# Linear attention and a SoLU feed-forward layer in one kernel: the first tile's hidden layer in float32, the maxima of k spread through DRAM, and a new order list

## The chip, the cores and the metric

The kernel runs on one core of one Trainium2 chip. The metric is the device time of one execution in microseconds, as the median over runs. Five engines work side by side and each executes its own instructions strictly in the order in which the kernel recorded them: PE (TensorE, matmuls), DVE (VectorE), ACT (ScalarE), POOL (GpSimd) and SP, which in this kernel only starts transfers. Engines wait for one another by semaphores. An instruction that waits holds up everything behind it on its own engine.

## The reference

```python
# attention; b, h, s, d = 8, 8, 576, 64
q_s = softmax(q, axis=-1)            # over d, with + 1e-9 in the denominator
k_s = softmax(k, axis=2)             # over the sequence: needs the maximum of k over s
kv  = einsum('bhsd,bhse->bhde', k_s, v)
out = einsum('bhsd,bhde->bhse', q_s, kv)

# feed-forward on x = out as [4608, 512]; d_ff = 1024
h    = x @ w_in
e    = exp(h - max(h)); sm = e / (sum(e) + 1e-9)
solu = h * sm
ln   = (solu - mean(solu)) / sqrt(var(solu) + 1e-6) * g_ln
y    = ln @ w_out
```

## The kernel before

The 4608 rows are 36 row tiles of 128: four from the first 512 rows of each batch, `(b, 0)` to `(b, 3)`, and one, `(b, 4)`, for every odd b, from the 64 remaining rows of two batches. All work is written as generators that yield between small steps.

For a batch b, `keys(b)` (key `K`) takes the maximum of k over the sequence: pairwise maxima on DVE (`khalf`, `ktop`), four float32 transposes on PE (`turned`), a reduction on DVE (`col`, a column of 128 x 4 numbers: the maximum for each of the 512 head and feature pairs). `col` must then reach all 128 partitions. Four more transposes of a broadcast `col` on PE (`wide`) and a copy on ACT (`kb`) do that. Then `km - kb` in two halves of heads and `kr - kb` for the last 64 rows (POOL, or DVE where the order list says so), exp on ACT, the float32 products k^T v on PE (`kv`, L386 and L391), a normalisation, and a split into a high and a low float16 part (`bd`). `queries(b, ...)` (`Qba`, `Qbc`) makes the softmax of q, its high and low part `qhl`, and a transposed copy `qT` by a DMA transpose from SP.

For a row tile, `attend` (`x`) multiplies `bd` and `qT` on PE and splits the result into float16 parts `xT` (high on ACT, low on DVE). `hidden` (`h`) multiplies with the high and low parts of `w_in` (`wi`): three float16 products for each of four blocks of 128 and each of two halves, 24 matmuls of 128x512. The maximum `top` (DVE, L550), exp `e` (ACT), `h*e` (DVE), mean, the high and low parts `u` and their transpose `uT` (a DMA transpose from SP), and the variance follow. `project` (`o`) multiplies `uT` with `wo`, 24 more matmuls, and stores.

The weights arrive as float64 words. `weight_in` (`w`) turns them into float32 `iw`; `weights_in_scaled` (`W`) takes the maximum of the column sums through PE (`wide_in`), makes a power of two, `s_in`, and writes the four blocks of `wi` (high on ACT, low on DVE, L280). `weight_out` (`y`) and `weights_out_scaled` (`Z`) do the same for `wo` (L321). `P` is a warm-up: four matmuls on idle data.

What sets the order is `ORDER`, a list of keys written out in one string. Each key advances its generator by one step; `.v` gives that step to DVE instead of its usual engine, and `*n` repeats it. So the list fixes the order on all engines, SP included, and the engine of the steps that have a choice. PSUM holds two `h` tiles, three of the tag "att" (`turned`, `wide`, `kv`, `x`) and one `o`. Number suffixes in the names below are buffers: `xT0_2` belongs to tile (0, 2), `kb2` to batch 2.

Of the kernel before, what the change touches and what calls it, by code (L numbers as in the profile page):

```python
# [8 lines left out]
F32 = mybir.dt.float32  # L9
# [8 lines left out]
P = 128  # L18

BUFS = 12, 4, 2  # L20
ORDER = (
# [77 lines left out]
def linear_attention_solu_ffn(ctx: ExitStack, tc: tile.TileContext, q, k, v, w_in, w_out, g_ln, out):  # L99
# [13 lines left out]
    C = 4  # L113
# [42 lines left out]
    def cast(eng, out, x):  # L156
        if eng is nc.scalar:
            eng.copy(out, x)  # L158
        else:
            eng.tensor_copy(out, x)  # L160

    def largest(x, wide, name):

        nc.tensor.transpose(wide, x.broadcast_to([P, P]), ident)
# [572 lines left out]
```

## Time and profile before

| | us |
|---|---|
| median of 3 runs (lowest to highest) | 475.32 (474.86 to 476.75) |
| the profiled execution, its own time | 477.42 |
| its span from first to last instruction | 475.6 |
| around the span | 1.8 |
| PE, DVE, ACT, POOL busy | 445.4, 342.7, 283.5, 208.8 |

A duration of a matmul in the profile includes its way through the array, and matmuls overlap. What one costs the engine is the distance from its start to the next start. In the tables of stages, the granted clock of PE is 1.00 at full speed and 0.50 at half.

### The profile page before, as it was taken

Reading aid. Unit: us, or ns where it says so; the run is one execution under the profiler, and the core shown is the slowest. Engines: PE = TensorE matmul, PEld = TensorE weight load, DVE = VectorE, ACT = ScalarE, POOL = GpSimd, SP = SyncE. Lnnn points to the kernel's source line nnn. Section 1 sums busy time; section 2 is a strip of 40 time slices with the busy share of each in tenths; the row PEclk is TensorE's granted clock in tenths of the full one; section 3 lists DMA queues with packets and bytes.
Section 4 is the critical chain, followed back from the end, with each engine's and each line's share of the span. In section 5 each row is a group of like instructions: output and inputs, shape, how many; then the busy total and the mean of one; then the engine's idle time right before and its main releaser. Section 6 shows DMA issues by size and latency. Waiting matters only on the chain.

```text
span 475.6 us, 8323 instructions
## 1 busy us (share of the span) xinstructions
PE 445.4 (94%) x3150; PEld 224.3 (47%) x3150; DVE 342.7 (72%) x596; ACT 283.5 (60%) x472; POOL 208.8 (44%) x308
## 2 busy tenths in 40 slices
PE   4367989999999999999899999999999999999997
PEld 1243444455445445544454454645454444444454
DVE  3989999979988898768888877656787655531610
ACT  1687899777657676845564657575575365441420
POOL 3222595395849526742742346541664411121210
PEclk9555999999999999999999999999999999999999
DMA  8899979198898878498729952959434462351062
GB/s 260 263 269 289 237 194 233 36 245 154 216 191 170 198 205 158 75 239 184 180 65 251 221 126 52 212 140 219 111 74 91 81 134 68 73 104 45 12 145 88
DMA packets 159240, 74.99 MB, mean 158 GB/s; under 512 B 127840, under 2 KB 152672, under 8 KB 159200
## 3 DMA queue, kind: packets, MB, share of 16 engines
q1 hardware_dynamic: 159200, 74.47, 67.1%
q8 instruction: 24, 0.39, 0.3%
q14 instruction: 16, 0.13, 0.1%
HBM read 36.70 MB, written 9.44 MB: 97 GB/s over the span
## 4 chain that ended last, share of the span: by engine, by line
PE 77%; DVE 7%; DMA 7%; ACT 4%; issue 2%; SPq 2%; POOL 1%; DVEq 0%; ACTq 0%
PE o L617 35%; PE h L543 33%; PE x L519 3%; PE kv L386 3%; DMA qT<-qhl 3%; DMA w_in<-in_moe_w_in_dram 2%; DMA km<-in_k_dram 2%; DVE top L550 1%; DVE gw L253 1%; PE wide L339 1%; DVE u L579 1%; PE kv L391 1%; DMA v<-in_v_dram 1%; PE turned L332 1%; ACT e L586 1%
## 5 line engine op out<-in xcount | busy, mean ns | idle before, releaser
L543 PE MATMUL h<-wi,xT 128*128 128x512 f16 x864 | 200.7, 381 | 3.5 <-ACT e L586 3.5
L617 PE MATMUL o<-wo,uT 128*128 128x512 f16 (+1 forms) x888 | 198.6, 373 | 0.0
L543 PEld LDWEIGHTS <-xT 128*128 128x128 f16 x864 | 84.5, 98 | 103.9 <-issue 6.3
L617 PEld LDWEIGHTS <-uT 128*128 128x128 f16 x888 | 86.0, 98 | 96.8
L550 DVE TENSOR_REDUCE top<-h 128x1 f32<-128x1024 f32 x36 | 43.9, 1218 | 31.4 <-PE h L543 31.1
L579 DVE SCALAR_TENSOR_TENSOR u<-h,nmu,u 128x1024 f16<-128x1024 f32 x36 | 45.9, 1277 | 21.1 <-ACT u L577 20.8
L572 DVE SCALAR_TENSOR_TENSOR h<-h,ph,e 128x1024 f32<-128x1024 f32 x36 | 46.2, 1286 | 10.8 <-POOL ph L569 6.7
L586 ACT ACTIVATE e<-h,nmu 128x1024 f32<-128x1024 f32 x36 | 40.0, 1110 | 15.2 <-DVE u L579 15.0
L452 POOL TENSOR_TENSOR qhl<-qm,qhl 128x1024 f16<-128x1024 f32 (+1 forms) x13 | 26.3, 2020 | 34.3 <-ACT qhl L158 28.2
L577 ACT ACTIVATE u<-h,nmu 128x1024 f16<-128x1024 f32 x36 | 40.0, 1112 | 1.0
L552 ACT ACTIVATE nm<-top,hs 128x1 f32<-128x1 f32 x32 | 9.4, 293 | 51.9 <-DVE top L550 51.7
L556 ACT ACTIVATE e<-h,nm,hs 128x1024 f32<-128x1024 f32 x32 | 38.4, 1201 | 0.8
L566 POOL TENSOR_TENSOR p<-pi,mone 128x1 f32<-128x1 f32 x36 | 22.5, 624 | 33.0 <-DVE pi L563 31.3
L627 ACT ACTIVATE os<-o,rr 128x512 f32<-128x512 f32 (+1 forms) x25 | 16.8, 674 | 29.1 <-PE o L617 20.4
L574 ACT ACTIVATE nmu<-s 128x1 f32<-128x1 f32 x36 | 7.3, 202 | 43.9 <-DVE h L572 43.7
L447 POOL TENSOR_TENSOR qm<-qm,qrec 128x1024 f32<-128x1024 f32 (+1 forms) x12 | 22.4, 1868 | 23.2 <-DVE qrec L445 18.2
L436 POOL TENSOR_TENSOR qm<-qm,qnmx 128x1024 f32<-128x1024 f32 (+1 forms) x15 | 29.5, 1969 | 3.7 <-DVE qnmx L434 3.7
L563 POOL TENSOR_SCALAR pi<-am 128x1 f32<-128x1 f32 x20 | 6.5, 323 | 51.6 <-DVE am L560 47.6
L599 POOL TENSOR_TENSOR r<-var,mhalf 128x1 f32<-128x1 f32 x36 | 21.0, 583 | 12.9 <-DVE var L596 12.2
L528 DVE SCALAR_TENSOR_TENSOR xT<-x,xT 128x512 f16<-128x512 f32 x36 | 24.3, 677 | 2.4 <-ACT xT L526 2.4
L386 PE MATMUL kv<-vm,km 128*64 128x65 f32 x512 | 18.5, 234 | 6.0 <-ACT km L369 6.0
L560 POOL TENSOR_SCALAR am<-nm 128x1 f32<-128x1 f32 x19 | 7.1, 373 | 37.8 <-ACT nm L552 37.4
(131 smaller groups left out, 555.4 us busy)
## 6 DMA issues: line engine op xcount, KB each, us to landing
v<-in_v_dram SPq DMA_DIRECT2D x32, 256.0 KB, 3.6
out_dram<-os SPq DMA_DIRECT2D x31, 256.0 KB, 3.2
km<-in_k_dram SPq DMA_DIRECT2D x7, 1024.0 KB, 7.0
qm<-in_q_dram SPq DMA_DIRECT2D x7, 1024.0 KB, 6.0
w_in<-in_moe_w_in_dram SPq DMA_DIRECT2D x8, 512.0 KB, 8.2
w_out<-in_moe_w_out_dram SPq DMA_DIRECT2D x8, 512.0 KB, 5.6
out_dram<-os SPq DMA_DIRECT2D x10, 128.0 KB, 2.4
qm<-in_q_dram SPq DMA_DIRECT2D x2, 512.0 KB, 4.3
```

What stands on the lines that cost most here:

```text
L386: nc.tensor.matmul(o, km[:, h + i, c], vm[:, h + i, c], start=(h == 0 and c == 0), stop=False)
L436: on(nc.gpsimd).tensor_tensor(x, x, wide(nmx), op=ALU.add)
L452: on(nc.gpsimd).tensor_tensor(lo, x, hi, op=ALU.subtract)
L528: nc.vector.scalar_tensor_tensor(xT[:, 1], acc, 1.0 / QS, xT[:, 0], op0=ALU.mult, op1=ALU.subtract)
L543: nc.tensor.matmul(h[:, ns], xT[:, t, kc], wi[:, s, kc, ns], start=(i == 0), stop=(i == len(terms) - 1))
L550: nc.vector.tensor_reduce(top, h, axis=AX.X, op=ALU.max, negate=True)
L556: nc.scalar.activation(e, h, AF.Exp, bias=nm, scale=hs, accum_out=z)
L572: nc.vector.scalar_tensor_tensor(h, h, ph, e, op0=ALU.mult, op1=ALU.mult, accum_out=s1)
L577: nc.scalar.activation(u[:, 0], h, AF.Identity, bias=nmu)
L579: nc.vector.scalar_tensor_tensor(u[:, 1], h, nmu, u[:, 0], op0=ALU.add, op1=ALU.subtract)
L586: nc.scalar.activation(e, h, AF.Square, bias=nmu, accum_out=s2)
L617: nc.tensor.matmul(o, uT[:, j, f], wo[:, s, f, cols], start=(f == 0 and j == 0 and s == 0), stop=(f == NF - 1 and j == 1))
```

## The change

Three things change.

The first row tile, `(0, 0)`, keeps its `xT` as one float32 tile, written by one scaled copy on ACT, and its `h` is 8 float32 matmuls with `iw` (in the order 3, 0, 2, 1 of the blocks, a step after each block) instead of 24 float16 ones with `wi`. It takes `kv`'s inverse scale alone for `hs`.

From batch 2 on, `col` goes to a DRAM tile `line` (512 floats, written element by element), and `kb` is read from it with a broadcast over the partitions. Both transfers are started by SP, and the second waits for the first. `wide` and its copy are gone for these six batches.

The order list is another one throughout. With it, the two parts of `qT` may come in either order.

```diff
+FIRST = 3, 0, 2, 1
+WHOLE = 1
+SPREAD = 2
 ORDER = (
-    "LQ0*2 Q0a.v LK0 Q0b Q0a Q0b.v LK0 V03 K0*2 Q0a LK0 K0 w3 V03 K0 w3 Q0a P Q0b P K0 V00.v P Q0a Q0c.v "
...
+    "LQ0*2 LK0 Q0a*2 Q0b.v LK0 Q0c.v LK0 w3 Q0a.v Q0a V03.v K0*3 Q0a.v Q0b P K0 Q0b.v Q0a V03 K0 Q0b w3 "
...
+    hbm = ctx.enter_context(tc.tile_pool(name="hbm", bufs=1, space=bass.MemoryType.DRAM))
...
+    def cast_scaled(eng, out, x, scale):
+        if eng is nc.scalar:
+            eng.activation(out, x, AF.Copy, scale=scale)
+        else:
+            eng.tensor_scalar(out, x, scale, None, op0=ALU.mult)
...
         nc.vector.tensor_reduce(col, turned, axis=AX.X, op=ALU.max)
         yield
+        if b >= SPREAD:
+            line = hbm.tile([NP * P], F32, name=f"line{b}", tag="line", bufs=2)
+            nc.sync.dma_start(out=line.rearrange("(n p) -> p n", p=P), in_=col)
+            yield
+            kb = sb.tile([P, H, D], F32, name=f"kb{b}", tag="kb", bufs=1)
+            nc.sync.dma_start(out=kb.rearrange("p h d -> p (h d)"), in_=line.unsqueeze(0).broadcast_to([P, NP * P]))
+            yield kb
+            return
         wide = ps.tile([P, NP, P], F32, name=f"wide{b}", tag="att", bufs=3)
...
+        if row_tile in whole:
+            xT = xT_of[row_tile] = sb.tile([P, NP, P], F32, name=f"xT{name}", tag="xT", bufs=XB)
+            cast_scaled(on(nc.scalar), xT, acc, 1.0 / QS)
+            yield
+            return
...
+        if row_tile in whole:
+            for i, kc in enumerate(FIRST):
+                for n in range(NB):
+                    ns = slice(n * 512, (n + 1) * 512)
+                    nc.tensor.matmul(h[:, ns], xT[:, kc], iw[kc][:, ns], start=(i == 0), stop=(i == NP - 1))
                 yield
-        hs = hs_of[("rest", row_tile[0] // 2) if row_tile[1] == C else row_tile[0]]
+            hs = kv_of[row_tile[0]][1]
+        else:
...
     tiles[-2:] = tiles[:-3:-1]
+    whole = tiles[:WHOLE]
```

ACT at the first tile, before: `xT0_0` stands behind all four column sums (`junk_in`) and a step on q, and the four blocks of `wi` follow. Here h of the first tile needs both.

```order
L266 ACTIVATE junk_in2_309,iw_sum_93<-iw2_262 128x1024
L266 ACTIVATE junk_in3_315,iw_sum_93<-iw3_157 128x1024
L266 ACTIVATE junk_in1_317,iw_sum_93<-iw1_280 128x1024
L158 CAST qhl0_2_353<-qm0_97 128x8x2x64
L526 ACTIVATE xT0_0_362<-x0_0_328 128x512
L158 COPY vm_76<-v1_3_321 128x8x64
L278 ACTIVATE wi_67<-iw0_188,s_in_371 128x1024
```

ACT at the same place now, with the first tile's scaled copy written by `cast_scaled` (L169):

```order
L277 ACTIVATE junk_in2_325,iw_sum_95<-iw2_218 128x1024
L169 ACTIVATE xT0_0_344<-x0_0_327 128x512
L277 ACTIVATE junk_in1_347,iw_sum_95<-iw1_290 128x1024
L163 CAST qhl0_1_358<-qm0_99 128x8x2x64
L551 ACTIVATE xT0_1_389<-x0_1_371 128x512
L289 ACTIVATE wi_69<-iw0_186,s_in_399 128x1024
```

The copy moved ahead of the last column sum. On PE the first two of the eight float32 matmuls stand ahead of `wide_in`, on which `s_in` and so `wi` depend, and the other six behind x of the second tile:

```order
L568 MATMUL h0_0_365<-iw3_166,xT0_0_344 128x512 x2
L175 MATMUL wide_in_368<-ident_88,m1_in_356 128x128
L539 LDWEIGHTS bd0_82
L539 MATMUL x0_1_371<-qT0_0_194,bd0_82 64x128
...
L568 MATMUL h0_0_365<-iw0_186,xT0_0_344 128x512 x2
L568 MATMUL h0_0_365<-iw2_218,xT0_0_344 128x512 x2
L568 MATMUL h0_0_365<-iw1_290,xT0_0_344 128x512 x2
```

Before, `wide_in` and x of the second tile stood ahead of all of h. SP in batch 2, before:

```order
L474 DMA_TRANSPOSE qT1_2_1137<-qhl1_2_1041 128x16x128
L192 DMA qm2_1181<-in_q_dram 128x8x256
L582 DMA_TRANSPOSE uT1_1_1186<-u1_1_1117 128x16x128
L198 DMA v3_3_1261<-in_v_dram 128x2x256
L198 DMA v3_1_1280<-in_v_dram 128x2x256
```

And now:

```order
L494 DMA_TRANSPOSE qT1_2_1077<-qhl1_1_997 128x16x128
L203 DMA qm2_1100<-in_q_dram 128x8x256
L350 DMA line2_1114<-col2_1085 128x4x1
L353 DMA kb2_1157<-line2_1114 128x512
L615 DMA_TRANSPOSE uT1_1_1159<-u1_1_1079 128x16x128
L663 DMA out_0_dram<-os0_10_1047 128x512
```

The two new transfers came in between the load of q for batch 2 and the transpose for tile (1, 1); `kb2` waits on SP for `line2`. DVE ahead of h of tile (1, 2), before:

```order
L579 SCALAR_TENSOR_TENSOR u1_1_1117<-h1_1_866,nmu1_1_1107,u1_1_1117 128x1024
L560 TENSOR_SCALAR am1_0_1188<-nm1_0_1158 128x1
L528 SCALAR_TENSOR_TENSOR xT1_2_1183<-x1_2_1139,xT1_2_1183 128x512
L590 TENSOR_SCALAR z11_1_1208<-z1_1_1063,p1_1_1100 128x1
L569 TENSOR_TENSOR ph1_0_1212<-p1_0_1202,hs1_908 128x1
L434 TENSOR_REDUCE qnmx2_0_1214<-qm2_1181 128x16
```

And now:

```order
L612 SCALAR_TENSOR_TENSOR u1_1_1079<-h1_1_836,nmu1_1_1067,u1_1_1079 128x1024
L165 COPY vm_78<-v2_1_981 128x8x64
L453 TENSOR_REDUCE qnmx2_0_1174<-qm2_1100 128x16
L602 TENSOR_TENSOR ph1_0_1182<-p1_0_1136,hs1_759 128x1
L553 SCALAR_TENSOR_TENSOR xT1_2_1167<-x1_2_1140,xT1_2_1167 128x512
```

The low part of `xT1_2` moved behind a copy of v, the row maxima of q of batch 2 (which need its load) and the factor `ph1_0` from POOL.

More of the change, by code (lines that the diff above doesn't have):

```diff
@@ L463, in parts @@
         def parts():
-            if c0 % 2 == 0:
-                hl_of[b] = sb.tile([P, 2, H, 2, D], F16, name=f"qhl{b}_{c0}", tag="qhl", bufs=1)
+            if (b, c0 // 2) not in hl_of:
+                hl_of[b, c0 // 2] = sb.tile([P, 2, H, 2, D], F16, name=f"qhl{b}_{c0 // 2}", tag="qhl", bufs=1)
+            hl = hl_of[b, c0 // 2]
             if n == 1:
-                return (hl_of[b][:, c0 % 2, :, i] for i in range(2))
-            return (hl_of[b][:, :, :, i].rearrange("p c h d -> p h c d") for i in range(2))
+                return (hl[:, c0 % 2, :, i] for i in range(2))
+            return (hl[:, :, :, i].rearrange("p c h d -> p h c d") for i in range(2))
         yield from q_softmax(x[:, :, 0] if n == 1 else x, parts, H * n, f"{b}_{c0}")
-        if c0 % 2 == 0:
-            qT_of[b, c0] = sb.tile([P, 2, H, P], F16, name=f"qT{b}_{c0}", tag="qT", bufs=2)
-            qT_of[b, c0 + 1] = qT_of[b, c0]
+        if (b, c0) not in qT_of:
+            c = c0 // 2 * 2
+            qT_of[b, c] = qT_of[b, c + 1] = sb.tile([P, 2, H, P], F16, name=f"qT{b}_{c}", tag="qT", bufs=2)
         nc.sync.dma_start_transpose(
             out=qT_of[b, c0][:, cs].rearrange("p c h k -> p (c h) k"),
-            in_=hl_of[b][:, cs].rearrange("p c h t d -> p (c h t d)"),
+            in_=hl_of[b, c0 // 2][:, cs].rearrange("p c h t d -> p (c h t d)"),
         )
@@ L537, in hidden @@
         h = ps.tile([P, DF], F32, name=f"h{name}", tag="h", bufs=2)
-        terms = [(kc, t, s) for kc in range(NP) for t, s in ((0, 0), (1, 0))] + [(kc, 0, 1) for kc in range(NP)]
-        for i, (kc, t, s) in enumerate(terms):
-            for n in range(NB):
-                ns = slice(n * 512, (n + 1) * 512)
-                nc.tensor.matmul(
-                    h[:, ns], xT[:, t, kc], wi[:, s, kc, ns], start=(i == 0), stop=(i == len(terms) - 1)
-                )
-            if i % 2 == 1:
-                yield
-        hs = hs_of[("rest", row_tile[0] // 2) if row_tile[1] == C else row_tile[0]]
+        if row_tile in whole:
[3 more added lines that the diff above has]
+                    nc.tensor.matmul(h[:, ns], xT[:, kc], iw[kc][:, ns], start=(i == 0), stop=(i == NP - 1))
+                yield
+            hs = kv_of[row_tile[0]][1]
+        else:
+            terms = [(kc, t, s) for kc in range(NP) for t, s in ((0, 0), (1, 0))] + [(kc, 0, 1) for kc in range(NP)]
+            for i, (kc, t, s) in enumerate(terms):
+                for n in range(NB):
+                    ns = slice(n * 512, (n + 1) * 512)
+                    nc.tensor.matmul(
+                        h[:, ns], xT[:, t, kc], wi[:, s, kc, ns], start=(i == 0), stop=(i == len(terms) - 1)
+                    )
+                if i % 2 == 1:
+                    yield
+            hs = hs_of[("rest", row_tile[0] // 2) if row_tile[1] == C else row_tile[0]]
         top = sm.tile([P, 1], F32, name=f"top{name}", tag="htop")
```

145 rows, old and new, of the table ORDER are left out of this document.

## The prediction

> **What bounds the kernel now.** I read the page first, then the stages, then PE's rows in order of time.
>
> ```profile
> PE 445.4 (94%) x3150; PEld 224.3 (47%) x3150; DVE 342.7 (72%) x596; ACT 283.5 (60%) x472; POOL 208.8 (44%) x308
> ...
> PEclk9555999999999999999999999999999999999999
> ```
> ```profile
> 0.00:40.00 40.00, 19.01 (x130) 10.12 (x130) 29.60 (x52) 22.52 (x34) 12.40 (x15) 0.65 0.96 272
> 40.00:60.00 20.00, 18.70 (x118) 9.53 (x119) 18.58 (x25) 16.27 (x24) 7.34 (x7) 0.86 1.00 246
> 60.00:83.00 23.00, 20.59 (x190) 10.62 (x188) 22.31 (x45) 22.65 (x39) 17.06 (x27) 1.00 0.87 210
> 83.00:143.00 60.00, 60.00 (x439) 30.47 (x437) 52.91 (x90) 40.14 (x69) 37.91 (x50) 1.00 0.76 170
> 143.00:440.00 297.00, 294.96 (x2108) 146.87 (x2107) 209.90 (x374) 173.01 (x293) 129.03 (x197) 1.00 0.62 139
> ```
> A row of the stages gives the stretch, then busy us of PE, PEld, DVE, ACT and POOL, the granted clock, DMA share and GB/s. From 83 to 440 us PE is idle for 2.0 us in 357. So the end is where PE becomes full, plus PE's work from there, plus the few waits. Before 83 us DVE and ACT are the full ones (22.3 and 22.7 of 23 us), and PE fills holes with warm-up matmuls.
>
> ```profile
> 34.86 1.89 PE L672 MATMUL warm_up<-bd 128*128 128x512 f16 x4
> ...
> 40.59 1.11 PE L332 MATMUL turned<-ident,ktop 128*128 128x128 f32 x4 [1.99 <-DVE ktop L361]
> ...
> 43.53 6.46 PE L543 MATMUL h<-wi,xT 128*128 128x512 f16 x24
> ```
> ```profile
> 78.78 4.48 PE L543 MATMUL h<-wi,xT 128*128 128x512 f16 x20 [0.57 <-ACT e L586]
> 83.09 5.34 PE L617 MATMUL o<-wo,uT 128*128 128x512 f16 x24
> ...
> 89.13 0.60 PE L332 MATMUL turned<-ident,ktop 128*128 128x128 f32 x4
> 89.57 2.75 PE L617 MATMUL o<-wo,uT 128*128 128x512 f16 x12
> ```
> A row is start and length; matmuls overlap, so a price is the step from one start to the next. At full clock four float32 128x128 matmuls take 0.44 us (89.13 to 89.57), 0.11 each; 20 of 128x512 in float16 take 4.31 (78.78 to 83.09), 0.216 each, 24 of them 5.18.
>
> The profiled execution took 477.42 us, 475.6 of span and 1.8 around it; it is 2.1 above the median of the runs, 475.32. I add the changes in the span to the median.
>
> **Part 1, the maxima through DRAM: what leaves PE.** Six batches lose four `wide` transposes each, and ACT six copies.
>
> ```profile
> L339 PE MATMUL wide<-ident,col 128*128 128x128 f32 x32 | 5.9, 315 | 2.1 <-DVE col L335 2.1
> L342 ACT COPY kb<-wide 128x512 f32<-128x512 f32 x8 | 4.6, 577 | 3.2 <-PE wide L339 3.2
> ```
> ```profile
> 234.59 0.65 PE L339 MATMUL wide<-ident,col 128*128 128x128 f32 x4 [1.27 <-DVE col L335]
> ```
> That is 24 x 0.11 = 2.64 us of PE, all on the path, since PE is full there (2.2 of it behind the first h of tile (1,2), see part 3). The third row is a wait on PE that goes with the transposes: `wide` of batch 6 stands in PE's order ahead of its `col`, 1.27 us. Nothing replaces it in that queue. The copies, 6 x 0.58 = 3.5 us of ACT, lie beside PE's work and bring nothing.
>
> **Part 2, the trip that replaces them.** `line` writes 512 single floats, `kb` reads 256 KB, and SP waits between the two. No row shows either; the nearest:
>
> ```profile
> v<-in_v_dram SPq DMA_DIRECT2D x32, 256.0 KB, 3.6
> ...
> km<-in_k_dram SPq DMA_DIRECT2D x7, 1024.0 KB, 7.0
> ...
> out_dram<-os SPq DMA_DIRECT2D x10, 128.0 KB, 2.4
> ...
> uT<-u SPq DMA_TRANSPOSE x36, 4.6
> ...
> gl<-in_moe_g_ln_dram SPq DMA_DIRECT2D x1, 4.0 KB, 5.7
> ```
> The last number is from issue to landing. `kb` is like `v`: 3.6, up to 7.0 behind a 1 MB load. `line` lies between the 2.4 of a small store and the 5.7 of `gl`, which also goes float by float but has twice as many; I take 4. With SP's two starts of about 0.5 the trip is 8.6 us (10.3 at the full price of `gl`; low 5.5, high 14). The Trainium skill (DMA: Bandwidth & Descriptors, Rules for kernel authors) says that a strided last dimension becomes one descriptor per element and should be rearranged, which speaks against this write; `gl` bears it out, and at its full price the sum below is 474.1.
>
> Who waits: the two halves of `km`, then `kv` on PE.
>
> ```profile
> L367 POOL TENSOR_TENSOR km<-km,kb 128x1024 f32<-128x1024 f32 x8 | 19.3, 2417 | 1.2 <-ACT kb L342 1.0
> ...
> L386 PE MATMUL kv<-vm,km 128*64 128x65 f32 x512 | 18.5, 234 | 6.0 <-ACT km L369 6.0
> L369 ACT ACTIVATE km<-km 128x1024 f32<-128x1024 f32 x16 | 16.9, 1054 | 7.1 <-POOL km L367 4.3 <-DVE km L367 2.8
> ```
> From `turned2` to `kv2` the new order has 64 matmuls of 0.216 and 32 small x: 14.8 us of PE (22.1 before). Counted the same way, batches 3 to 7 have 17.8, 15.6, 19.4, 21.8 and 27.7. Of this `col` with its place in DVE's queue takes some 2.7, a half's subtraction 2.4 and its exp 1.05: 6.1. So the trip may last 8.7 us in batch 2 and 9.5 in batch 4 before PE waits: I cost it at nothing, with nothing to spare; at 10.3 it would be 1.6 + 0.8 = 2.4. While SP waits for `line`, `uT1_1` and a store of `out` queue behind it; `uT` lands in 4.6 and each o stands at least 22 us of PE work after its h, so 6 us of delay is covered by that.
>
> **Part 3, the first tile's h and the new order up to tile (2,1).** The 24 float16 matmuls become 8 of float32. `kv` is 32 products a batch in the code and 512 rows in the trace, two rows a product; a full row of 128 columns costs 0.11, so a product of 512 columns is 2 x 0.44 = 0.88 us and the tile 7.0 instead of 5.2 (low 3.5, if one row did). PE has holes here, so the 1.8 is not on the path. What is: this h no longer waits for `wi`.
>
> ```profile
> 42.95 4.86 DVE L280 SCALAR_TENSOR_TENSOR wi<-iw,s_in,wi 128x1024 f16<-128x1024 f32 x4
> 47.73 1.28 DVE L251 TENSOR_SCALAR gw<-gw 128x1024 int32<-128x1024 int32 x2
> 50.04 1.22 DVE L550 TENSOR_REDUCE top<-h 128x1 f32<-128x1024 f32 x1 [1.03 <-PE h L543]
> ...
> 57.11 1.27 DVE L579 SCALAR_TENSOR_TENSOR u<-h,nmu,u 128x1024 f16<-128x1024 f32 x1
> ```
> ```profile
> 81.41 2.83 DVE L321 SCALAR_TENSOR_TENSOR wo<-gw,gs,wo 128x512 f16<-128x512 f32 x4
> ```
> ```profile
> 34.00:36.00 2.00, 2.00 (x16) 1.12 (x17) 1.51 (x2) 2.00 (x5) 0.00 (x0) 0.50 1.19 311
> ...
> 44.00:46.00 2.00, 2.00 (x7) 0.77 (x6) 2.00 (x3) 2.00 (x3) 0.00 (x0) 0.55 0.99 220
> 46.00:48.00 2.00, 2.00 (x11) 0.93 (x10) 2.00 (x3) 2.00 (x3) 0.00 (x0) 1.00 0.94 238
> ```
> The warm-up ahead of it ends at 36.8. Two products at half clock: 40.5; `wide_in` and x of the second tile: 42; six at full clock: 47.3, against 50.0. DVE has three of the four `wi` steps ahead of `top` and is free at 47.5. So `top` starts 2.5 us earlier. From there to the first `wo` step DVE holds 33.8 us of rows (each at its mean in the groups) instead of 33.0, and such rows run in 0.91 to 0.93 of their sum (the four `wi` steps took 4.86 for 4 x 1.27): 0.7 back. `wo` starts at 79.6 instead of 81.4.
>
> Then the new order loads DVE. From the first `wo` to xT of tile (1,2) its rows sum to 28.0 us instead of 23.3, to xT of (2,1) 59.7 instead of 50.9: POOL's steps on q, two lo parts and a scaling among them, move to DVE.
>
> ```profile
> L452 DVE TENSOR_TENSOR qhl<-qm,qhl 128x1024 f16<-128x1024 f32 x4 | 4.8, 1212 | 0.0
> ```
> ```profile
> 104.36 0.69 DVE L528 SCALAR_TENSOR_TENSOR xT<-x,xT 128x512 f16<-128x512 f32 x1 [1.02 <-ACT xT L526]
> ...
> 106.81 1.22 DVE L434 TENSOR_REDUCE qnmx<-qm 128x16 f32<-128x1024 f32 x1 [0.56 <-DMA qm<-in_q_dram]
> ```
> ```profile
> 106.67 5.34 PE L543 MATMUL h<-wi,xT 128*128 128x512 f16 x24
> ```
> That xT now also stands behind this row of `qnmx` and its load. 79.6 + 0.93 x 28.0 = 105.6, and with 1 us of waits as before it (1.02) 106.6: h of (1,2) starts where it did, though PE alone could have been there 2 us sooner. At (2,1) DVE is at 79.6 + 55.5 = 135.1 plus waits, PE at 137.1. So the gain of the start is spent: -0.1.
>
> **Sum.** -0.1 (start and DVE), -2.2 (20 transposes behind that place), -1.3 (batch 6's wait): -3.6, 471.7 us. Queues: SP gets 12 issues more, 6 us in the span; POOL loses 19 us of rows of its 209, which brings nothing.
>
> **The rivals.**
> 1. DVE stays behind: of its 7.1 idle us from 83 to 143 (52.9 of 60 busy) I allow 2 to remain by (2,1). If 4.5 do, PE waits 2.5 more: 474.2, no measurable change. For it: 97% busy ahead of 83 us, and 8.8 us added.
> 2. The trip is long: `line` queued behind `qm`'s 1 MB (7.0) and `kb` at 5 make 13 us, and batches 2, 4 and 3 hold PE for 4.3 + 3.5 + 1.3 = 9.1: 480.8, slower. It decides from about 12 us on (6 us of waits). Against it: SP waits for `col2` after that load has started.
> 3. Half clock through the whole float32 tile: six products take 10.6, not 5.3, everything up to tile (2,1) follows DVE 5.3 later: 477.0. The clock was 0.50 at 34 to 36 us with PE full and rose near 45.5, 5 us after work without a break began at 40.59; here it begins near 35. The Trainium skill (TensorE: Matmul & The Clock Gate, Part 1) gives one busy window of about 3.4 us for the rise; by it this rival falls, but the trace took longer, so it keeps a chance.
> 4. The float32 tile gains nothing since the start is DVE's anyway: this is nearly my forecast, and without its 2.5 the time is 474.2.
>
> **How the numbers follow.** The runs before spread by 0.4%, so 0.5%, 2.4 us, is what can be told: 472.9 and 477.7. Forecast 0.58 (468 to 474, 0.05 of it above 472.9), rivals 1 and 4 together 0.20 (0.02 below 472.9), rival 3 0.08 (0.03 above 477.7), rival 2 0.12 (0.01 within), a larger gain 0.02. Faster 0.53 + 0.02 + 0.02 = 0.57 (the forecast's 0.53, the rivals' 0.02, the larger gain's 0.02); slower 0.11 + 0.03 = 0.14; the rest, 0.29, is no change. The range runs from 467.5, where PE keeps the 2 us by which it could be sooner at (1,2), the 1 us of waits there is gone and so is the rest of PE's 2.0 idle us up to 440 (0.7), to 478.0, which takes in rival 3 and leaves out most of rival 2.
>
> **What would show it.** Right: no `wide` on PE after batch 1; PE at or above 99% from the first o; h of the first tile ending near 47 us; first `wo` on DVE near 79.6; `kb` landing under 9 us after `col`, and PE waiting under 1 us at each `kv`. Wrong: h of (1,2) far from 106.6, rows of PE with waits on `xT` up to 140 us (rival 1), on `km` (rival 2), or a granted clock of 0.50 past 43 us (rival 3).

## The result, and the profile after

The changed kernel took 527.44 us (525.55 to 529.48, 4 runs) against 475.88 (474.86 to 476.75, 4 runs) for the kernel before on the same chip: a ratio of 1.107, with a 95% interval of 1.104 to 1.111. It is 11% slower; the forecast was 471.7 with a range up to 478.0. The profiled execution has a span of 523.8 us. PE's row of the page, and the clock that it was granted:

```profile
PE 454.1 (87%) x3118; PEld 224.9 (43%) x3118; DVE 351.1 (67%) x620; ACT 280.9 (54%) x467; POOL 199.4 (38%) x282
...
PEclk9999999978998999879979998899996999999999
```

The stages (stretch; busy us of PE, PEld, DVE, ACT, POOL; clock; DMA share; GB/s):

```profile
0.00:40.00 40.00, 21.91 (x166) 11.03 (x167) 30.39 (x59) 24.76 (x36) 13.85 (x16) 1.00 1.00 288
...
83.00:143.00 60.00, 52.72 (x386) 27.42 (x385) 48.67 (x88) 33.31 (x57) 27.44 (x34) 0.91 0.72 162
143.00:440.00 297.00, 262.02 (x1846) 129.14 (x1845) 201.96 (x356) 155.00 (x261) 114.05 (x159) 0.94 0.64 134
```

From 83 to 440 us PE is now idle for 42.3 of 357 us where it was idle for 2.0, and its clock, 1.00 before, is 0.91 and 0.94. The holes cost twice: after each of 3 us or more the matmuls run at half clock for some us. Six stretches at 0.50, 47.8 us in all, begin in these holes or just behind them. PE is busy for 29.7 us of them, which at half clock is 14.8 us lost (an estimate). Against the run with the short trip below (PE idle for 2.2 us, span 467.4) that makes 40.1 + 14.8, so 55 of the 56.4 us between the spans. The start is better than it was, with a clock of 1.00 up to 40 us in this execution where it was 0.65.

The two transfers of the trip in the list of DMA issues (count, size, median us from issue to landing):

```profile
kb<-line SPq DMA_DIRECT2D x6, 256.0 KB, 4.5
...
line<-col SPq DMA_DIRECT2D x6, 2.0 KB, 10.5
```

The waits (us in total, times, longest), of the engines and then of SP's queue:

```profile
DVE km L386 <- DMA kb<-line: 26.4, 3, 12.3
ACT km L388 <- POOL km L386: 25.8, 4, 9.8
ACT os L660 <- DMA out_dram<-os: 25.7, 3, 13.4
...
PE o L650 <- DVE os L658: 16.2, 2, 9.2
...
POOL km L386 <- DMA kb<-line: 13.9, 2, 8.6
```
```profile
SPq L353 <- DMA line<-col: 46.1, 5, 11.3
```

Two kinds of waits begin at the trip. DVE and POOL wait for `kb`, and SP waits for `line`, with stores of `out` behind it, for which ACT then waits. Of the 25.7 us in the row of that wait 13.4 lie at 512 us, at the kernel's end, where the run without the trip has them too; 10.5 are in batch 3. Batch 3 shows both kinds, in rows of time: SP, DVE, ACT, PE.

```profile
146.97 0.53 SPq L350 DMA_DIRECT2D line<-col  x1
147.55 0.50 SPq L209 DMA_DIRECT2D v<-in_v_dram  x1
157.90 0.34 SPq L353 DMA_DIRECT2D kb<-line  x1
158.33 0.38 SPq L663 DMA_DIRECT2D out_dram<-os  x1
158.80 4.76 SPq L615 DMA_TRANSPOSE uT<-u  x1
```
```profile
144.78 0.68 DVE L346 TENSOR_REDUCE col<-turned 128x4 f32<-128x512 f32 x1
...
149.43 1.28 DVE L612 SCALAR_TENSOR_TENSOR u<-h,nmu,u 128x1024 f16<-128x1024 f32 x1
163.03 1.23 DVE L386 TENSOR_TENSOR km<-km,kb 128x1024 f32<-128x1024 f32 x1 [12.32 <-DMA kb<-line]
```
```profile
163.84 0.69 ACT L660 ACTIVATE os<-o,rr 128x512 f32<-128x512 f32 x1 [10.54 <-DMA out_dram<-os]
```
```profile
164.58 2.72 PE L650 MATMUL o<-wo,uT 128*128 128x512 f16 x6 [6.04 <-ACT os L660]
```

SP starts `line` at 146.97 and can start `kb` only at 157.90. The store behind it starts at 158.33; ACT, which wants that store's buffer for the next `os` (there are two), waits 10.5 us, and PE waits for ACT. DVE has 5 us of other rows behind `col` and then stands 12.3 us at the subtraction, with other tiles' steps behind it. The six matmuls after PE's hole take 2.5 us (164.58 to 167.09), 0.42 each, twice the 0.216 of full clock.

PE's holes of over half a us sum to 41.9 us: 12.9 at `kv`, 25.9 at `o`, 3.1 at `x`. Followed back from row to row, some 18 of them come from SP being held: the store above (6.0), a load of v in batch 7 for which ACT waits 10.45 us (9.2 on PE), and a transpose for qT in batch 4 (3.1). The other 24 come from a late `kb`: those at `kv`, and those at `o` in batches 5 and 6 (10.7), since `os` stands there behind the subtraction or its exp.

### The profile page after: what moved, and what is told of

It reads as the page before. It is cut to its first block, busy times and chain, and to the rows that moved or that the text cites. A ratio compares the mean times of both kernels' runs of the same rounds, so it can differ in the third digit from the quotient of the medians.

```text
span 523.8 us, 8269 instructions
## 1 busy us (share of the span) xinstructions
PE 454.1 (87%) x3118; PEld 224.9 (43%) x3118; DVE 351.1 (67%) x620; ACT 280.9 (54%) x467; POOL 199.4 (38%) x282
## 4 chain that ended last, share of the span: by engine, by line
PE 52%; DMA 15%; DVE 13%; ACT 8%; issue 7%; POOL 3%; SPq 2%; ACTq 0%; POOLq 0%; DVEq 0%
PE o L650 27%; PE h L576 19%; DMA line<-col 6%; PE kv L405 2%; DMA kb<-line 2%; DMA w_in<-in_moe_w_in_dram 2%; PE x L539 2%; DVE u L612 2%; POOL km L386 2%; DMA qm<-in_q_dram 2%; DMA km<-in_k_dram 1%; DVE h L605 1%; DMA uT<-u 1%; DVE top L583 1%; ACT km L388 1%
## 5 line engine op out<-in xcount | busy, mean ns | idle before, releaser
L650 PE MATMUL o<-wo,uT 128*128 128x512 f16 (+1 forms) x888 | 204.8, 384 | 26.0 <-DVE os L658 16.2
L576 PE MATMUL h<-wi,xT 128*128 128x512 f16 x840 | 194.7, 382 | 4.0 <-ACT e L619 4.0
L650 PEld LDWEIGHTS <-uT 128*128 128x128 f16 x888 | 87.7, 100 | 130.1 <-issue 37.4
L576 PEld LDWEIGHTS <-xT 128*128 128x128 f16 x840 | 82.3, 99 | 102.0 <-issue 8.1
L599 POOL TENSOR_TENSOR p<-pi,mone 128x1 f32<-128x1 f32 x36 | 25.6, 712 | 57.6 <-DVE pi L596 56.2
L660 ACT ACTIVATE os<-o,rr 128x512 f32<-128x512 f32 (+1 forms) x25 | 16.6, 665 | 41.6 <-DMA out_dram<-os 25.7
L388 ACT ACTIVATE km<-km 128x1024 f32<-128x1024 f32 x16 | 16.8, 1053 | 33.5 <-POOL km L386 25.8
L386 POOL TENSOR_TENSOR km<-km,kb 128x1024 f32<-128x1024 f32 x9 | 22.6, 2508 | 31.8 <-issue 17.9
L405 PE MATMUL kv<-vm,km 128*64 128x65 f32 x512 | 21.1, 247 | 14.1 <-ACT km L388 14.1
L471 POOL TENSOR_TENSOR qhl<-qm,qhl 128x1024 f16<-128x1024 f32 (+1 forms) x11 | 22.2, 2017 | 28.3 <-ACT qhl L163 15.3
L632 POOL TENSOR_TENSOR r<-var,mhalf 128x1 f32<-128x1 f32 x36 | 22.5, 626 | 19.6 <-DVE var L629 18.8
```

The costliest lines, as they stand in the source:

```text
L386: on(nc.gpsimd).tensor_tensor(km[:, hs], km[:, hs], wide, op=ALU.subtract)
L405: nc.tensor.matmul(o, km[:, h + i, c], vm[:, h + i, c], start=(h == 0 and c == 0), stop=False)
L576: nc.tensor.matmul(h[:, ns], xT[:, t, kc], wi[:, s, kc, ns], start=(i == 0), stop=(i == len(terms) - 1))
L599: nc.gpsimd.tensor_tensor(p, pi, mone, op=ALU.pow)
L650: nc.tensor.matmul(o, uT[:, j, f], wo[:, s, f, cols], start=(f == 0 and j == 0 and s == 0), stop=(f == NF - 1 and j == 1))
```

## The experiments

### Which part: the order, or the trip

The new order and the float32 tile without the trip (`SPREAD = 2` becomes `SPREAD = 8`), and the old order and old first tile with the trip alone:

```diff
 kernel before, in tops_of:
+        if b >= SPREAD:
+            line = hbm.tile([NP * P], F32, name=f"line{b}", tag="line", bufs=2)
+            nc.sync.dma_start(out=line.rearrange("(n p) -> p n", p=P), in_=col)
...
+            yield kb
+            return
```

> The changed kernel with the trip taken out: all eight batches turn the maxima by PE and spread them by `wide` transposes and an ACT copy, as batches 0 and 1 do. The new order and the float32 first tile stay. If the trip makes the loss (the first theory), what is left is the new start, which in the changed kernel's trace has the first `wo` 5.5 us and h of (1,2) 5.1 us earlier than before: 475.9 - 5 = 471, between 467 and 476. If the new order (or the float32 tile) makes a good part of the loss (the rival), 490 or more.

> The kernel before, with its own order and its first tile in two halves of 16 bits, with nothing but the trip through DRAM put in for batches 2 to 7 (the steps stand where the `wide` transposes and the copy stood). First theory (the trip alone makes the loss): 520 to 545, since the changed kernel's start gives 5 us back and its order at least knew of the trip. Rival (the new order makes the loss): under 490.

Without the trip 474.43 us (ratio 0.996, 0.993 to 0.998); with the trip alone 554.67 (1.164, 1.159 to 1.169). The trip makes the whole loss. It costs the old order 78 us, more than I expected, and the new one 53. (The run with the old order has the old first tile too, so the order and the tile aren't told apart here.)

### What of the trip: SP held, or the chain of kb

The chain of `kb`, the K chain below, runs from `kb` over the subtraction and the exp to `kv`. Here `kb` is made the old way, and the trip is made too, at the same places in SP's queue, but nobody reads what it brings:

```diff
         wide = ps.tile([P, NP, P], F32, name=f"wide{b}", tag="att", bufs=3)
+        if b >= SPREAD:
+            line = hbm.tile([NP * P], F32, name=f"line{b}", tag="line", bufs=2)
+            nc.sync.dma_start(out=line.rearrange("(n p) -> p n", p=P), in_=col)
...
+        if b >= SPREAD:
+            idle = sb.tile([P, IDLE], F32, name=f"idle{b}", tag="idle", bufs=1)
+            nc.sync.dma_start(out=idle, in_=line[0:IDLE].unsqueeze(0).broadcast_to([P, IDLE]))
         kb = sb.tile([P, H, D], F32, name=f"kb{b}", tag="kb", bufs=1)
         nc.scalar.copy(kb.rearrange("p h d -> p (h d)"), wide.rearrange("p n k -> p (n k)"))
```

> The changed kernel with both ways at once: k's maxima are spread by `wide` transposes and the ACT copy (so nothing of the K chain waits for DRAM), while SP still writes `line` and reads it back, from the same places in its queue, into a tile that nobody reads. If the time is lost because SP is held some 10 us per batch with the stores of `out` and the uT transfers behind it (theory H1): 500 or more, with the o stalls of batches 3 and 5 to 7 still there. If it is lost in the chain of kb to the subtraction, exp and kv (theory H2): under 482, with the o stalls gone. From the stalls of the changed kernel (about 27 us at o, about 14 us at kv and x) I expect 495, nearer H1.

503.32 us (1.058, 1.052 to 1.064), somewhat over the 495 expected. A trip that nobody but SP waits for costs 29 us against the same order without it. In its trace the row that pays in batch 3 is the store again:

```profile
153.56 0.34 SPq L358 DMA_DIRECT2D idle<-line  x1
154.00 0.38 SPq L662 DMA_DIRECT2D out_dram<-os  x1
```
```profile
159.29 0.69 ACT L659 ACTIVATE os<-o,rr 128x512 f32<-128x512 f32 x1 [8.68 <-DMA out_dram<-os]
```

But the stores aren't the main thing behind SP's wait. PE's idle time from 83 to 440 us is 22.4 us here and 2.3 without the trip. Followed back, 11.9 of it stand behind loads of v that SP started late (3.75 in batch 2, 0.76 in batch 5, 7.36 in batch 7), 6.3 behind stores (4.18 in batch 3, 2.12 in batch 4), 2.0 behind a transpose for qT, and 2.2 at `wide`, as without the trip. Of the stalls at o that were expected in batches 3 and 5 to 7, those of 3 and 7 are there. The load of v in batch 7:

```profile
364.96 0.33 SPq L358 DMA_DIRECT2D idle<-line  x1
365.38 2.66 SPq L210 DMA_DIRECT2D v<-in_v_dram  x2
```
```profile
370.73 0.62 ACT L164 COPY vm<-v 128x512 f32<-128x512 f32 x1 [9.03 <-DMA v<-in_v_dram]
```

Then both transfers issued from POOL (`nc.gpsimd.dma_start` for `nc.sync.dma_start`), so that SP is free:

> The changed kernel with both transfers of the trip issued from POOL instead of SP: the trip stays long (512 pieces of 4 bytes), the K chain still waits for it, but the stores of `out` and the uT transfers do not stand behind it on SP; POOL's own small steps (pi, p, r, and the additions of q) do. The run with the trip unused gave 503.3 against 474.4 without a trip, so holding SP alone costs 29 us, and the K chain on top of it 24. If the two add up (theory A), freeing SP gives 474 + 24 = 498, plus what POOL's steps lose. If either one alone is enough to stop PE, since o and kv stand in one PE queue (theory B): 505 to 525. If POOL's steps behind the wait (p of each tile stands ahead of h) matter as much as the stores (theory C): over 525.

530.77 us (1.116, 1.112 to 1.119), no better than from SP. Here POOL waits for `line`, and its landing, issued this way, took 12.2 us (the same write from SP took 10.5, 9.4 and 8.4 in three runs):

```profile
POOL kb L353 <- DMA line<-col: 61.5, 6, 12.3
```

That is above the 525 of theory B, and 1.7 us more for `line` in six batches can make 10 of it, so B and C aren't told apart. A is out, the two losses don't add up: freeing SP gains nothing while the chain is long and another engine is held instead. What the long K chain would cost with no queue held wasn't tried, since some engine must wait for `line` to issue `kb`; its own share stays open.

### Why `line` takes 10.5 us

First the layout: each partition's four maxima side by side, 128 pieces of 16 bytes, and two by two, 256 of 8.

```diff
-            nc.sync.dma_start(out=line.rearrange("(n p) -> p n", p=P), in_=col)
+            nc.sync.dma_start(out=line.rearrange("(p n) -> p n", p=P), in_=col)
```
```diff
+            nc.sync.dma_start(
+                out=line.rearrange("(a p j) -> p a j", a=2, j=2), in_=col.rearrange("p (a j) -> p a j", a=2)
+            )
```

> The changed kernel with `line` written in rows of four neighbouring maxima (128 pieces of 16 bytes where there are 512 of 4 bytes). kb's columns then hold each other's maxima; what is subtracted from k's columns cancels in the softmax, so only the layout of the trip differs. If line's 10.5 us come from the number of its pieces: landing 3 to 5 us, the trip 15.5 falls to about 9 us, and the time to 485 to 505. If they come from waiting behind other transfers, or from a fixed price of a write to DRAM that is read again: landing still about 10 us, time within 1% of 527.

> The changed kernel with `line` written in 256 pieces of 8 bytes. By the number of pieces (128 pieces landed after 2.3 us, 512 after 10.5): 2.3 + 128 x 8.2 / 384 = 5.0 us landing, trip about 9.5 us. The prediction had the trip hidden up to about 12 us: then the time is 468 to 473, as with 16 bytes. If each us of the trip costs from the start (straight line from 469.7 at 6.1 us to 527.4 at 15.5): about 490.

With 16 bytes 469.66 us (0.986, 0.982 to 0.991), faster than the kernel before; with 8 bytes 479.27 (1.006, 1.003 to 1.010). `line` landed after 2.3 and 4.0 us, sooner than the 3 to 5 and the 5.0 expected, and with 16 bytes the time fell further than to the 485 to 505 expected. In 8-byte pieces the trip, 8.4 us by the medians, already costs 9.6 us more than one of 6.1 (about 1 us of it lies ahead of the trip in the profiled executions, where the first `col` that takes it ends at 96.1 and 95.0 us). Of the two times expected, the straight line's 490 is too high and the prediction's 468 to 473 too low.

Then what about the pieces: few of 4 bytes, many of 16, and few of 4 bytes that lie apart, all in the kernel with the trip unused.

```diff
 128 of 4 bytes:
+            nc.sync.dma_start(out=line.rearrange("(n p) -> p n", p=P), in_=col[:, 0:1])
 512 of 16 bytes:
+                out=line.rearrange("(n p j) -> p n j", p=P, j=4), in_=flat[:, 0 : 4 * NP].rearrange("p (n j) -> p n j", j=4)
 128 of 4 bytes, apart:
+            w = 4 << (b - SPREAD) % 3
+            nc.sync.dma_start(out=line[0 : P * w].rearrange("(p j) -> p j", j=w)[:, 0:1], in_=col[:, 0:1])
```

> The new order with `wide` for all batches, and a trip that nobody waits for but SP, as in the run with the trip unused; but `line` takes only the first column of the maxima: 128 pieces of 4 bytes, and 128 columns are read back. If the number of pieces makes the landing time: 2 to 2.5 us, and the time is 473 to 478. If pieces of 4 bytes are slow in themselves (their size): 6 us or more, and the time over 485.

> New order, `wide` for all batches, and a trip that only SP waits for; `line` is 512 pieces of 16 bytes side by side in DRAM (16 columns of the column maxima of rows, `top`, a stand-in, instead of the maxima). With 128 pieces of 4 bytes the landing was 8.6 us, of 16 bytes 2.3, 256 of 8 bytes 4.0: the number of pieces is out as the cause. If small pieces that lie side by side get in each other's way (theory D: the time goes with how many pieces share one stretch of DRAM: 16 of 4 bytes, 8 of 8, 4 of 16 in 64 bytes): 2 to 4 us landing. If a piece's size and the number together make it (a fixed price per small piece per transfer engine): 5 us or more.

> As the run with 128 pieces of 4 bytes, but the pieces lie apart in DRAM: 16 bytes from one to the next in batches 2 and 5, 32 in batches 3 and 6, 64 in batches 4 and 7 (and only one value of `line` is read back). Theory D (neighbours get in each other's way): landing about 2.3 us at 16 bytes, 1.5 to 2.3 at 32 and 64. Rival (a write of 4 bytes is slow in itself, wherever it goes): 8 to 10 us at all three. If the stretch they share is larger than 64 bytes, it falls with the distance but is not yet low at 16.

The rows of `line` in the three lists of DMA issues, in this order:

```profile
line<-col SPq DMA_DIRECT2D x6, 0.5 KB, 8.6
```
```profile
line<-ktop SPq DMA_DIRECT2D x6, 8.0 KB, 3.7
```
```profile
line<-col SPq DMA_DIRECT2D x6, 0.5 KB, 2.1
```

My first reading, a price per piece, is refuted: a quarter of the pieces took 8.6 us, hardly less than all 512 in the three runs from SP (8.4 to 10.5), and as many pieces as in the changed kernel, of 16 bytes, 3.7 (2.7 to 6.8 over the batches). So is "4 bytes are slow": 16 bytes apart they landed after 3.6 and 2.5 us, at 32 after 2.2 and 2.0, at 64 after 1.4 and 1.7. What counts is how densely small pieces lie in DRAM. The times follow: 501.68 us (1.056, 1.051 to 1.061), 473.62 (0.995, 0.993 to 0.997) and 474.62 (0.997, 0.994 to 1.000).

Nor is it a queue. In batch 4 of the changed kernel, from the issue at 200.4 to 202 us, and from there to the landing at 212.1, the DMA queues show:

```profile
DMA packets 528, 0.00 MB, mean 1 GB/s; under 512 B 528, under 2 KB 528, under 8 KB 528
...
line<-col SPq DMA_DIRECT2D x1, 2.0 KB, 11.7
```
```profile
DMA packets 1, 0.02 MB, mean 2 GB/s; under 512 B 0, under 2 KB 0, under 8 KB 0
```

All pieces have left by 202 us (the last ends 1.3 us after the issue), and for 10 us nothing moves but one instruction fetch, before the landing is reported. The Trainium skill (DMA: Bandwidth & Descriptors, Anatomy of one DMA) puts most of a fixed price of some 2 us, for a transfer started by GpSimd, down to the confirmation from the target memory, and (Specifications) says that transfers under 512 bytes are read, modified and written back. The wait after the last piece agrees with the first, at five times its size; that neighbours are written back one after the other would be a cause, but what happens inside the memory no run shows.

### From which length the trip costs

The old order with the 16-byte line (the edits of the second and the third experiment together), and the changed kernel with `kb` read at once from values that need no `line`:

```diff
-            line = hbm.tile([NP * P], F32, name=f"line{b}", tag="line", bufs=2)
-            nc.sync.dma_start(out=line.rearrange("(n p) -> p n", p=P), in_=col)
             yield
             kb = sb.tile([P, H, D], F32, name=f"kb{b}", tag="kb", bufs=1)
-            nc.sync.dma_start(out=kb.rearrange("p h d -> p (h d)"), in_=line.unsqueeze(0).broadcast_to([P, NP * P]))
+            nc.sync.dma_start(out=kb.rearrange("p h d -> p (h d)"), in_=k[b, 0, 0:H].rearrange("h d -> (h d)").unsqueeze(0).broadcast_to([P, NP * P]))
```

> The kernel before with its own order and its own first tile, and the trip of batches 2 to 7 with `line` in 128 pieces of 16 bytes. If a trip of 6 us is hidden in the old order too, it saves the 24 `wide` transposes and their ACT copies: 470 to 475. If the order found for the trip is what hides it (the old order lets SP reach `line` late and asks for kb soon, as its 554.7 with the long trip against 527.4 suggests): 478 to 495.

> The changed kernel without `line`: kb is filled by the same kind of transfer (256 KB, one row of 2 KB to all partitions) from 512 values of k itself, which need no waiting; what is subtracted from a column of k cancels in its softmax, so no output changes. Only the second transfer of the trip is left, about 4 us. Theory: what a batch loses is the time from the end of `col` to the landing of kb, less the distance that the order leaves between `col` and the first subtraction (in the run without a trip 6.9, 5.2, 4.7, 5.2, 11.3, 10.0 us for batches 2 to 7). With the 16-byte line the landing came 7.1, 7.7, 5.5, 6.8, 7.3, 6.1 us after `col`, which loses 0.2 + 2.5 + 0.8 + 1.6 = 5 us; without `line` nothing is lost: 469.7 - 5 = 465. Rival (a trip of 6 us is hidden already, the loss begins at some point above it): 468 to 471.

506.98 us (1.066, 1.061 to 1.071) in the old order, more than I expected, where the new one with the same `line` takes 469.66. Without `line` 468.56 (0.984, 0.979 to 0.988), which can't be told from 469.66. So a trip of 6 us is all but hidden in the new order: from 83 to 440 us PE is idle for 2.2 us with it and for 0.4 without `line`. In the old order the trip isn't hidden, and it's longer there as well: SP comes to `line` 4.2 us after `col` in batch 3 and 2.0 in batch 4.

The reason can be read as a distance. Between `col` and the first subtraction an order leaves so many us of other rows; the trip may be as long, and beyond that DVE or POOL stands. From the traces, batches 2 to 7, us (to about 0.1):

| | b2 | b3 | b4 | b5 | b6 | b7 | over, sum |
|---|---|---|---|---|---|---|---|
| new order, no trip: `col` to subtraction | 6.9 | 5.2 | 4.7 | 5.2 | 11.3 | 10.0 | |
| changed kernel: `col` to `kb` (b3: to the subtraction) | 15.5 | 17.6 | 15.0 | 12.2 | 17.4 | 15.3 | 49.7 |
| 8 bytes | 9.9 | 9.5 | 7.6 | 8.2 | 10.1 | 8.1 | 13.2 |
| 16 bytes | 7.1 | 7.7 | 5.5 | 6.8 | 7.3 | 6.1 | 5.1 |
| old order, before: `col` to subtraction | 4.8 | 2.3 | 1.6 | 2.9 | 4.3 | 2.6 | |
| old order, 16 bytes | 6.7 | 11.5 | 8.6 | 7.6 | 6.4 | 7.5 | 29.8 |

Measured, against the kernel without `line` (468.6), the changed kernel is 58.9 us longer, 8 bytes 10.7, 16 bytes 1.1; the old order with 16 bytes is 31.4 over the kernel before. The sums 49.7, 13.2, 5.1 and 29.8 come in the right order and near the size, but as a price the rule isn't shown. It gives nothing for the trip unused, which lost 29 us through SP's queue, and the half clock after the holes (14.8 us in the changed kernel) isn't in it. Without `line` I expected 465. There SP comes late to `kb` in batches 3 and 5, and it lands 6.2 and 6.1 us after `col`, 1.9 over; so the rule's gain is 3.2 where 1.1 was measured, with intervals of some 2 us to each side of both times.

### The float32 tile alone

The kernel before with float32 `xT` and `h` for the first tile, in the old order:

```diff
+        if row_tile in whole:
+            for i, kc in enumerate(FIRST):
+                for n in range(NB):
+                    ns = slice(n * 512, (n + 1) * 512)
+                    nc.tensor.matmul(h[:, ns], xT[:, kc], iw[kc][:, ns], start=(i == 0), stop=(i == NP - 1))
+                yield
+            yield
+            yield
```

> The kernel before with nothing but the float32 first tile (its xT in one piece, 16 products of 0.43 us in place of 24, w_in's float32 copies in place of the halves), in the old order. The new order with float32 and without the trip gave 0.9956, 1.8 us less. If the float32 tile is what moved the start: its first h ends 2 to 5 us earlier than at 50.0 and the time is 472 to 474. If the new order moved it: the first h within 1.5 us of 50.0, and the time 475 to 476.5.

478.17 us (1.004, 1.002 to 1.007), above both ranges expected: alone it gains nothing, and why it is 2 us slower is open. The first h ends at 49.4 (50.0 before), since it stands behind `turned` and `wide` of batch 1 in PE's old order:

```profile
38.62 1.11 PE L340 MATMUL turned<-ident,ktop 128*128 128x128 f32 x4 [2.03 <-DVE ktop L369]
...
40.65 1.12 PE L347 MATMUL wide<-ident,col 128*128 128x128 f32 x4
41.56 7.81 PE L557 MATMUL h<-iw,xT 128*128 128x512 f32 x16
```

## Why the prediction was wrong, step by step

**What bounds it.** Right for the kernel with a short trip: with 16 bytes PE is busy 354.8 of the 357 us from 83 to 440, at a clock of 1.00.

```profile
PE 439.4 (94%) x3118; PEld 218.4 (47%) x3118; DVE 353.0 (76%) x620; ACT 280.8 (60%) x467; POOL 200.4 (43%) x282
...
PEclk9999999999999999999999999999999999999999
```

**Part 1, the transposes that leave PE.** Right in kind, somewhat low. With the trip short against no trip, in the same order, the time falls by 4.8 us (469.66 against 474.43; their intervals against the kernel before don't meet). The forecast had 2.2 + 1.3 = 3.5. All 24 transposes are 2.6 of the 4.8. The wait at `wide` of batch 6 is there in the new order too, and longer, 2.20 for 1.27:

```profile
272.46 0.65 PE L358 MATMUL wide<-ident,col 128*128 128x128 f32 x4 [2.20 <-DVE col L346]
```

"Nothing replaces it" is wrong, though. From 83 to 440 us PE is idle for 2.3 us without the trip and for 2.2 with the short one, where two waits of 1.04 came in. What goes with the wait is a stretch of 3.4 us at half clock behind it, some 1.7 us. The rest of the 4.8 isn't pinned down.

**Part 2, the price of the trip: the first step that failed.** `line` was put at 4 us, between a small store (2.4) and `gl` (5.7); it took 10.5. Neither neighbour is such a write: the store goes in rows, and `gl` reads DRAM in single floats. The upper end of the range, 14 us for the whole trip, didn't hold either: 15.5 in batch 2. `kb` was close, 4.5 for 3.6. The rule of the Trainium skill that I cited (DMA: Bandwidth & Descriptors, Rules for kernel authors), one descriptor for each element of a strided last dimension, pointed the right way. But the number of pieces isn't what was paid for, as the runs with 128 and 512 of them show.

**Part 2, the slack: the second.** I counted PE's work from `turned` to `kv` (14.8 us in batch 2) and took off 6.1 for `col`, one half's subtraction and its exp. For that first half the count holds: with 8 bytes `kb` landed 9.9 us after `col` in batch 2, over the 8.7 allowed, and the first half's `kv` still didn't wait. The second half isn't in the count. Its subtraction and exp stand behind other tiles' steps, and PE waited for it, 2.31 us there, and 1.04 with 16 bytes in batch 4, where the trip took 5.5 us and 9.5 were allowed:

```profile
110.00 1.15 PE L407 MATMUL kv<-vm,km 128*64 128x65 f32 x32
113.46 1.15 PE L407 MATMUL kv<-vm,km 128*64 128x65 f32 x32 [2.31 <-ACT km L390]
```
```profile
195.31 1.10 PE L405 MATMUL kv<-vm,km 128*64 128x65 f32 x32
197.46 1.15 PE L405 MATMUL kv<-vm,km 128*64 128x65 f32 x32 [1.04 <-ACT km L388]
```

And PE's `kv` isn't the first to wait: the subtraction stands in DVE's and POOL's queues with other tiles' steps behind it, and the distance to it is shorter (the table: 4.7 to 6.9 in batches 2 to 5). The point from which the trip decides lies between 6.1 and 8.4 us, not at 12.

**Part 2, SP's queue: the third.** "6 us of delay is covered" looked at uT's 22 us to its o. The stores of `out`, the loads of v and the transposes for qT in the same queue have no such distance: with two `os` buffers ACT waits for a store, 8.7 us in batch 3 even where the K chain is short, and for a load of v, 9.0 us in batch 7. The trip unused cost 29 us, and of PE's idle time in it 11.9 us stand behind loads, 6.3 behind stores and 2.0 behind a transpose.

**Rival 2** named the mechanism, with 0.12 and 480.8. It priced the trip at 13 us and let three batches pay 9.1, on PE alone; all six pay, in DVE's, POOL's, ACT's and SP's queues. The same trip is what the forecast assumed when `line` is written in 16-byte pieces: 6.1 us by the medians, under its 8.6, and 469.66 for 471.7. That agreement owes something to luck: the forecast gain was 3.6 us, and 6.5 were measured against the kernel before beside it, with errors on both sides, as the next step shows. (By its own terms, 2 + 1 + 0.7 below 471.7, the lower end of the range is 468.0, not 467.5.)

**Part 3, the start.** The price of the float32 tile holds: its 16 rows take 1.72 and 5.26 us (34.16 to 35.88, 36.70 to 41.96), 6.98 for 7.0.

```profile
34.16 1.88 PE L568 MATMUL h<-iw,xT 128*128 128x512 f32 x4
35.88 0.32 PE L175 MATMUL wide_in<-ident,m_in 128*128 128x128 f32 x1
36.14 0.64 PE L539 MATMUL x<-qT,bd 128*64 128x128 f16 x16
36.70 5.42 PE L568 MATMUL h<-iw,xT 128*128 128x512 f32 x12
41.96 0.60 PE L343 MATMUL turned<-ident,ktop 128*128 128x128 f32 x4
...
101.60 1.67 PE L576 MATMUL h<-wi,xT 128*128 128x512 f16 x7
```

Its end was put at 47.3 and came at 42.0. It starts at 34.2, 2.6 us ahead of the end of the warm-up from which the sum counted, and its first rows run at full clock (1.00 from 28 to 36 us; 0.50 in the old order with the same tile), which saves 2.0 more; the rest is in the rows between. The first `wo` starts at 75.9 (79.6 forecast). From there DVE keeps the forecast pace: h of (1,2) starts at 101.6 (106.6), 5.1 us earlier than before and 25.7 us after the first `wo`, 0.92 of the 28.0 us of rows. (The example given for a pace of 0.91 to 0.93, 4.86 us for 4 x 1.27, is 0.96.) So "the gain of the start is spent" failed by the start, mis-sized by 3.7 us, and not by the pace.

The time of the new order without the trip is only 1.8 us lower. In its trace h of (1,2) starts 4.5 us earlier than before (102.2), and the span is 2.9 us shorter (472.7 for 475.6): 1.7 us go at the half clock behind the wait at `wide`. The profiled execution of the kernel before was itself 1.2 us above the median that the 1.8 is measured from (477.42 for 476.20).

Rival 4 is right on the tile itself, which alone, in the old order, gains nothing; what the new order gains without the tile no run shows. Rival 1 didn't occur, since DVE kept its pace. Nor did rival 3: the tile ran at full clock. But in the run without the trip, with the same order, the clock is 0.50 up to 34.4 us, just before the tile starts at 34.6, so it came close.

## What to carry to other kernels

When a wait moves from PE to an in-order queue, measure the slack on that queue: from the producer to the first instruction that waits, with everything that stands behind it, loads and small stores among them. A transfer that no row of the trace resembles deserves a measurement before it is given a price, and a planner's order is only as good as that price: the same order was worth +11% or -1.4% by the layout of 2 KB. To pass a column between partitions through DRAM, write each partition's values side by side. In the runs here a column of `kb` then holds another column's maximum, which cancels in the softmax; what it costs to put them back in order, where a kernel needs that, no run shows.

## What the runs showed of the hardware

- 2 KB written to DRAM as 512 neighbouring pieces of 4 bytes landed after 10.5 us (9.4 and 8.4 in two other runs), as 256 of 8 bytes after 4.0, as 128 of 16 bytes after 2.3; 512 neighbouring pieces of 16 bytes after 3.7; 128 neighbouring pieces of 4 bytes after 8.6, the same 64 bytes apart after 1.4 to 1.7. In batch 4 of the changed kernel the pieces themselves had left 1.3 us after the issue.
- Issued from POOL instead of SP, the same 512 pieces landed after 12.2 us.
- In these traces, from 83 to 440 us, each hole of PE of 3 us or more had a stretch at a granted clock of 0.50 in it or behind it, as had some of 2.0 to 2.9 us; holes up to 1.7 us, with no larger one just before them, had none. Over 143 to 440 us the mean clock is 0.94 in the changed kernel and 1.00 with 16 bytes.
